# Nine small loads for the left-over rows of W_down in layer two, and fewer unread products in two norms

## The chip, the cores and the metric

The kernel runs on one core of one Trainium2 chip. The core has five engines that run side by side: PE (matrix products; loading its weights is listed apart as PEld), DVE (vector work), ACT (scalar functions and copies), POOL (here only set-up), and SP, which issues the transfers. Transfers run on the core's 16 DMA engines. The metric is the device time of one execution in microseconds; the time before is 730.42, the median of three runs (730.34 to 730.63).

## The reference

Two equal layers are computed, each of them an attention over a cached window and a gated MLP, for a batch of B = 4 with one token each. D = 640, 32 heads of 128, a window of 1024 keys, F = 1728.

```python
x = x + _A_ref(_layernorm(x), A_k_cache, A_v_cache, A_wq, A_wo)
x = x + _B_ref(_layernorm(x), B_W_gate, B_W_up, B_W_down)
x = x + _A_ref(_layernorm(x), A_k_cache, A_v_cache, A_wq, A_wo)
x = x + _B_ref(_layernorm(x), B_W_gate, B_W_up, B_W_down)
# _A_ref: q = x @ wq; softmax(q k^T / sqrt(128)) v over the last 1024 keys; @ wo
# _B_ref: gate = x @ W_gate; h = gate * (gate > 0) * (x @ W_up); h @ W_down
```

All of it is in float32. The weights and the caches are the same in both layers, and there is far more of them than the memory on the core can hold, so most of them are read twice.

## The kernel before

On the host, everything that is read is laid out in rows of 128 partitions: `heads` (q, k, v and o of the first heads), `kept` (those of the last heads), `mlp` (the MLP's weights) and `limbs` (the last 128 keys' values of head 17, cut into pieces of few partitions). A large tile, `store` (128 partitions by 50,624 columns of float32), takes them in turn.

**The loads.** `plan` is a list of loads, each with a layer, a row, a range of columns `lo` to `hi` and a place `to` in `store`. It is written out by hand and worked off in that order. `load()` issues every load at the list's head whose place is free; `live` keeps which columns are still to be read, and `free()` and `done()` call `load()` after each product that frees some. So the program fixes on SP one order of loads, each with the semaphores that it waits for: those of PE or ACT for its place, and one of the eight semaphores DMAHW0 to DMAHW7, which the loads take in turn. A load waits until the earlier load on its own semaphore has landed. SP works its list off in order, so a load that waits holds those behind it.

The `limbs` loads take five rows, or two, at a stride of four partitions. They fill the last 2048 columns of `store` (from 48,576), which `free(STORE - PART, STORE)` gives back after head 17.

**The MLP.** W_down has 1728 rows: three blocks of 512, one of 128, and 64 left-over rows. In `mlp` the left-over rows lie at `TAIL` as 128 partitions by 320 columns: the halves of the 64 rows stand above each other. In layer two the MLP comes by nine loads, with the borders in `cuts`. `forward()` works off `gate(3)`, then `gate(0)`, `gate(1)`, `gate(2)`, each a set of products with W_gate and W_up into `pp`, followed by ACT and DVE (`gated`) and by a transposition of h (`hidden`), and then `down(3)`, `down(0)`, `down(1)`, `down(2)` into y. `gate(3)` and `down(3)` are those of the last 192 columns of F: a block of 128 and the 64 left over. For these, `hidden(3)` turns h by PE into `ph` and copies it to `probs`, and `down(3)` does four products with the left-over rows, each on 64 partitions. At the end y is copied to `probs` and stored.

**The unread products.** `busy(n)` and `fill(n)` put products on PE whose results nobody reads; they do so only while `waits[0]` is true. `normalized()` sets it to true at its start, puts two by `busy` behind the sum of y and one by `fill` behind the mean. It is called four times: in `attention` and in `forward` of both layers.

Of the kernel before, what the change touches and what calls it, by code (L numbers as in the profile page):

```python
# [14 lines left out]
P = 128  # L15
KC = D // P
QUARTER = D // 4
# [44 lines left out]
STORE = 50624  # L62
# [7 lines left out]
FIRST, MOST = 32384, 16192  # L70
LAP = 3 * MOST
SPLIT, PART = 17, 2048
LIMBS = [(half + i, 5, 0, 1536) for i in range(4) for half in (0, 32)] + [(i, 2, 1536, PART) for i in range(4)]
RUNS = [(half, 20, 512 * s, 40 * s + 20 * (half > 0)) for s in range(3) for half in (0, 32)] + [(0, 8, 1536, 120)]

# [37 lines left out]
def decode_kernel(ctx: ExitStack, tc: tile.TileContext, x, source, out):  # L113
# [99 lines left out]
    to = stretch(1, hi, last, 0)  # L213
    for lo, hi in (last, near(last + 12800)), (near(last + 12800), heads_end):
        to = put(1, "heads", to if to + hi - lo <= STORE else 0, lo, hi)
    cuts = [0, 7040, 12160, GU0 + 3 * GU, WD1 + WD, MLP - 4 * D, MLP - 2 * D, MLP - D, MLP - QUARTER, MLP]
    for lo, hi in zip(cuts, cuts[1:]):
        to = put(1, "mlp", to if to + hi - lo <= STORE else 0, lo, hi)

    plan.reverse()  # L220

# [3 lines left out]
    def load():  # L225

        if not held:
            nc.sync.dma_start(out=first_q, in_=source["heads"][:, :HELD])
        while plan:
            layer, row, lo, hi, to = plan[-1]  # L230
            if any(live[to:STORE if row == "limbs" else to + hi - lo]):
                break
            plan.pop()
            if row == "limbs":
                live[to:STORE] = [lo == len(LIMBS) - 1] * PART
                p, n, a, b = LIMBS[lo]
                nc.sync.dma_start(out=store[p:p + 4 * n - 3:4, to + a:to + b], in_=source[row][p:p + 4 * n - 3:4, a:b])  # L237
                continue
            live[to:to + hi - lo] = [True] * (hi - lo)
            held.setdefault((layer, row), []).append((lo, hi - lo, to))  # L240
            nc.sync.dma_start(out=store[:, to:to + hi - lo], in_=source[row][:, lo:hi])
# [128 lines left out]
            nc.tensor.matmul(m[32 * g:32 * g + 32], sel_q, a, start=True, stop=True, tile_position=(0, 32 * g))  # L370
        return m

    def normalized():

        ysb, xc, sq = probs[:, :QUARTER], gates[:, :QUARTER], gates[:, QUARTER:2 * QUARTER]
        waits[0] = True
        nc.vector.tensor_reduce(su, y, axis=AX.X, op=ALU.add)
        nc.scalar.copy(ysb, y)
        busy(2)
        mu = mean(su)  # L380
        nc.vector.tensor_tensor(xc, ysb, mu.to_broadcast([P, QUARTER]), op=ALU.subtract)
        nc.scalar.activation(sq, xc, AF.Square, accum_out=ss)
        fill(1)
        nc.vector.transpose(xT, xc)
        return ss
# [140 lines left out]

    def attention(layer):
        gs = order[layer]
        rstd = deviation(normalized())
        table(AF.Exp)  # L530
        query(layer, gs[0], True)
        query_out(gs[0], rstd)
        query(layer, gs[1])
        query_turned(gs[0])
        go_on()
        query_out(gs[1], rstd)
        scores(layer, gs[0])
        query(layer, gs[2])
        softmax(gs[0])
        query_turned(gs[1])  # L540
        query_out(gs[2], rstd)
        for before, g, after, then in zip([None] + gs, gs, gs[1:] + [None], gs[2:] + [None] * 2):
            totals(g)
            turned()
            if layer == 0 and after is None:
                nc.scalar.copy(probs[:, QUARTER:QUARTER + 768], store[:, AHEAD[0]:AHEAD[1]])
                nc.scalar.copy(ps.rearrange("p j n -> p (j n)"), store[:, BACK[0]:BACK[0] + 1024])
                nc.scalar.copy(yy[:, QUARTER:3 * QUARTER], store[:, BACK[1] - 320:BACK[1]])
                free(*AHEAD)
            if before is not None:  # L550
                values_turned(before)
            if then is not None and before is not None:
                query(layer, then)
                query_out(then, rstd)
            if after is not None:
                scores(layer, after)
                softmax(after)
            else:
                table(AF.Sqrt)
            if then is not None:  # L560
                query_turned(then)

            if before is not None and not (layer == 0 and after is None):
                project(layer, before)
            values(layer, g, after is None)
        values_turned(gs[-1])
        if layer == 0:
            for i in range(2):
                nc.scalar.copy(banks[i][:, P:], away[:, 512 + 384 * i:896 + 384 * i])
            free(*AWAY)  # L570
            project(layer, gs[-2])
        fill(1)
        project(layer, gs[-1], True)

    def forward(layer):
        ss = normalized()
        gus, hTs = {}, {}

        def gate(j):
            n, groups = (P, 4) if j < 3 else (64, 3)  # L580
            at = GU0 + j * GU if j < 3 else 0
            gus[j] = pp[:, j % 2, :2 * P]
            for c in range(KC):
                for g in range(groups):
                    lo = at + (c * groups + g) * 2 * n
                    product(gus[j][32 * g:32 * g + 32], xT[:, 32 * c:32 * c + 32], layer, "mlp", lo, 2 * n,
                            start=c == 0, stop=c == KC - 1, tile_position=(0, 32 * g))
                    done(layer, "mlp", lo, 2 * n)

        def gated(j):  # L590
            n, p = (P, P) if j < 3 else (64, 96)
            gu = gus.pop(j)
            at = P * (j + 1) % 512
            a, b = gates[:p, at:at + n], probs[:, :P] if j < 3 else gates[:p, 3 * P:3 * P + n]
            nc.scalar.activation(a, gu[:p, :n], AF.Relu, scale=rstd[:p])
            nc.vector.scalar_tensor_tensor(b, gu[:p, n:2 * n], rstd[:p], a, op0=ALU.mult, op1=ALU.mult)
            return b

        def hidden(j, h):
            if j < 3:  # L600
                hTs[j] = gates[:, P * j:P * j + P].rearrange("p (f x) -> p f x", f=4)[:, :, :B]
                nc.vector.transpose(gates[:, P * j:P * j + P], h)
                return
            hTs[j] = probs[:, P:P + 2 * B].rearrange("p (f x) -> p f x", f=2)
            ph = bank(P).rearrange("p (f x) -> p f x", f=4)
            for g, lo, f in (0, 0, 0), (1, 64, 0), (2, 0, 1), (2, 64, 1):
                nc.tensor.matmul(ph[lo:lo + 64, f, :B], h, ident[:96, 32 * g:32 * g + B],
                                 start=True, stop=True, tile_position=(0, lo))
            nc.vector.tensor_copy(hTs[j], ph[:, :2, :B])

        def down(j, last=False):
            for f in range(4 if j < 3 else 1):
                lo = WD1 + j * WD + f * D if j < 3 else WD0
                for g in range(4):
                    product(y[32 * g:32 * g + B], hTs[j][:, f], layer, "mlp", lo + g * QUARTER, QUARTER,
                            start=False, stop=last and f == 3, tile_position=(0, 32 * g))
                done(layer, "mlp", lo, D)
                if j == 3:
                    fill(1)
                elif not (last and f > 1):  # L620
                    busy(1)
                if j == 0 and f == 1:
                    fill(2)
            if j == 3:
                for g in range(4):
                    r = slice(64 * (g // 2), 64 * (g // 2) + 64)
                    product(y[32 * g:32 * g + B], hTs[j][r, 1], layer, "mlp", TAIL + g % 2 * QUARTER, QUARTER,
                            start=False, stop=False, rows=r, tile_position=(r.start, 32 * g))
                done(layer, "mlp", TAIL, 2 * QUARTER)

        gate(3)
        waits[0] = layer == 0
        rstd = deviation(ss)
        go_on()
        fill(1)
        h = gated(3)
        for j, j1 in (3, 0), (0, 1), (1, 2):
            gate(j1)
            hidden(j, h)
            fill(1)  # L640
            h = gated(j1)
        down(3)
        down(0)
        hidden(2, h)
        if layer == 0:
            nc.scalar.copy(away[:, :512].rearrange("p (j n) -> p j n", j=2), pp[:, :, 256:])
            for i in range(2):
                nc.scalar.copy(away[:, 512 + 384 * i:896 + 384 * i], banks[i][:, P:])
            live[AWAY[0]:AWAY[1]] = [True] * 1280
        down(1)  # L650
        down(2, last=True)

# [61 lines left out]
```

## Time and profile before

| | us |
|---|---|
| median of three runs | 730.42 |
| the profiled execution | 730.35 |
| its span, from the first to the last instruction | 728.5 |
| attention's last load (128x12672) issued | 660.03 |
| first MLP load of layer two issued | 666.03 |
| last products begin | 724.81 |
| store issued | 725.87 |

In what follows, a row of the timeline has a start, a length, the engine, the line, the operation and its tiles, a count, and in brackets how long the engine stood idle before it and what ended that. "SPq" is SP's list of transfers. A piece of the chain has a start, a length and what the end of the program was waiting for. A row of the waits has the total, the number of times and the longest. A row for a stretch has its borders, its length, PE's busy time with a count, the granted clock of PE as a share of full speed, the mean busy share of the 16 DMA engines (packets are counted where they start, so it can pass 1) and GB/s. Products in float32 have two records each.

### The profile page before, as it was taken

Reading aid. Unit: us, or ns where it says so; the run is one execution under the profiler, and the core shown is the slowest. Engines: PE = TensorE matmul, PEld = TensorE weight load, DVE = VectorE, ACT = ScalarE, POOL = GpSimd, SP = SyncE. Lnnn points to the kernel's source line nnn. Section 1 sums busy time; section 2 is a strip of 40 time slices with the busy share of each in tenths; the row PEclk is TensorE's granted clock in tenths of the full one; section 3 lists DMA queues with packets and bytes.
Section 4 is the critical chain, followed back from the end, with each engine's and each line's share of the span. In section 5 each row is a group of like instructions: output and inputs, shape, how many; then the busy total and the mean of one; then the engine's idle time right before and its main releaser. Section 6 shows DMA issues by size and latency. Waiting matters only on the chain.

```text
span 728.5 us, 8337 instructions
## 1 busy us (share of the span) xinstructions
PE 442.4 (61%) x3816; PEld 142.2 (20%) x3816; DVE 70.0 (10%) x215; ACT 54.2 (7%) x101; POOL 1.8 (0%) x11
## 2 busy tenths in 40 slices
PE   3545564644655475519878896465655556557576
PEld 1111111111111121103333241021111112102123
DVE  2010010000010000002111211001000010001011
ACT  2000000000000000001312210000000000000100
POOL 0000000000000000000000000000000000000000
PEclk9978787977778786759999999677777787859889
DMA  9999999999999999999999999999999999999997
GB/s 406 447 394 447 439 444 444 401 441 437 439 432 421 418 456 421 440 423 429 417 413 413 435 429 448 443 430 436 419 440 436 437 436 415 448 435 430 420 423 301
DMA packets 13482, 311.10 MB, mean 427 GB/s; under 512 B 1572, under 2 KB 1956, under 8 KB 7176
## 3 DMA queue, kind: packets, MB, share of 16 engines
q1 hardware_dynamic: 13440, 310.56, 99.2%
q8 instruction: 30, 0.49, 0.2%
q14 instruction: 4, 0.03, 0.0%
q10 hardware_dynamic: 8, 0.01, 0.0%
HBM read 310.49 MB, written 0.08 MB: 426 GB/s over the span
## 4 chain that ended last, share of the span: by engine, by line
DMA 77%; PE 20%; SPq 1%; issue 1%; DVE 0%; ACT 0%; DVEq 0%
DMA store<-in_heads 61%; PE ps L272 9%; DMA store<-in_kept 8%; DMA store<-in_mlp 8%; PE po L272 6%; PE m L272 2%; PE y L272 1%; PE pp L272 1%; PE pp L457 1%; PE m L428 1%; SPq L237 1%; PE po L486 0%; PE m L513 0%; PE m L504 0%; PE y L400 0%
## 5 line engine op out<-in xcount | busy, mean ns | idle before, releaser
L272 PE MATMUL po<-store,pT 128*16 128x512 f32 (+1 forms) x1024 | 155.8, 712 | 125.5 <-DMA store<-in_heads 118.8
L272 PE MATMUL ps<-store,qT 128*4 128x512 f32 (+3 forms) x996 | 147.5, 676 | 102.4 <-DMA store<-in_heads 81.1
L272 PEld LDWEIGHTS po<-store,pT 128*16 128x16 f32 x1024 | 32.1, 109 | 232.4 <-DMA store<-in_heads 122.4
L272 PEld LDWEIGHTS ps<-store,qT 128*4 128x4 f32 x996 | 29.5, 92 | 202.6 <-DMA store<-in_heads 92.0
L453 ACT ACTIVATE probs<-ps,nm 128x1024 f32<-128x1024 f32 x17 | 18.9, 1113 | 332.9 <-DVE nm L449 332.9
L272 PE MATMUL m<-store,xT 128*32 128x512 f32 (+4 forms) x150 | 29.5, 598 | 23.2 <-DMA store<-in_heads 23.2
L449 DVE TENSOR_REDUCE nm<-ps 128x1 f32<-128x1024 f32 x17 | 20.8, 1225 | 230.1 <-PE ps L272 230.1
L272 PE MATMUL y<-store,oT 128*4 128x160 f32 x512 | 22.0, 305 | 11.0 <-DMA store<-in_heads 9.8
L500 ACT COPY gates<-po 128x512 f32<-128x512 f32 x16 | 9.4, 586 | 259.7 <-PE po L272 259.7
L272 PE MATMUL pp<-store,xT 128*32 128x256 f32 (+3 forms) x322 | 20.1, 350 | 8.7 <-DMA store<-in_mlp 4.2
L466 DVE COPY pT<-pp 128x32 f32<-128x32 f32 x64 | 10.3, 185 | 135.9 <-PE po L272 117.3
L457 PE MATMUL pp<-sel_sb,probs 128*128 128x128 f32 x144 | 20.1, 286 | 0.0
L457 PEld LDWEIGHTS pp<-sel_sb,probs 128*128 128x128 f32 x144 | 17.8, 150 | 0.0
L506 DVE RECIPROCAL r<-m 128x16 f32<-128x16 f32 x18 | 4.6, 257 | 132.0 <-PE m L504 132.0
L272 PEld LDWEIGHTS y<-store,oT 128*4 128x4 f32 x512 | 12.3, 87 | 18.8 <-DMA store<-in_heads 10.1
L421 DVE TENSOR_SCALAR gates<-m,rstd 128x512 f32<-128x512 f32 (+2 forms) x18 | 12.4, 689 | 29.2 <-PE m L272 29.2
L272 PEld LDWEIGHTS pp<-store,xT 128*32 128x32 f32 x322 | 10.4, 109 | 17.0 <-DMA store<-in_mlp 7.6
L272 PEld LDWEIGHTS m<-store,xT 128*32 128x32 f32 x150 | 6.3, 116 | 35.7 <-DMA store<-in_heads 25.8
L428 PE MATMUL m<-sel_sb,gates 128*128 128x128 f32 x64 | 12.7, 324 | 0.0
L513 PE MATMUL m<-sel_sb,gates 128*128 128x128 f32 x72 | 11.7, 284 | 0.8 <-DVE gates L493 0.8
L428 PEld LDWEIGHTS m<-sel_sb,gates 128*128 128x128 f32 x64 | 7.9, 160 | 19.6 <-issue 19.1
L272 PE MATMUL y<-store,gates 128*4 128x160 f32 x192 | 9.8, 299 | 2.2 <-DMA store<-in_mlp 2.1
(82 smaller groups left out, 131.5 us busy)
## 6 DMA issues: line engine op xcount, KB each, us to landing
store<-in_heads SPq DMA_DIRECT2D x15, 7936.0 KB
store<-in_heads SPq DMA_DIRECT2D x3, 8096.0 KB
store<-in_heads SPq DMA_DIRECT2D x3, 7872.0 KB
store<-in_heads SPq DMA_DIRECT2D x2, 8032.0 KB
store<-in_heads SPq DMA_DIRECT2D x1, 8000.0 KB
store<-in_heads SPq DMA_DIRECT2D x1, 7424.0 KB
store<-in_heads SPq DMA_DIRECT2D x1, 7360.0 KB
store<-in_heads SPq DMA_DIRECT2D x1, 7168.0 KB
```

The costliest lines, as they stand in the source:

```text
L237: nc.sync.dma_start(out=store[p:p + 4 * n - 3:4, to + a:to + b], in_=source[row][p:p + 4 * n - 3:4, a:b])
L272: nc.tensor.matmul(out[:, a:z], by, t[rows, p:p + z - a], start=start and not a, stop=stop and z == n, **how)
L421: nc.vector.tensor_scalar(gates[:, :len(HEADS[g]) * P], qp.pop(g), rstd, SCALE, op0=ALU.mult, op1=ALU.mult)
L428: nc.tensor.transpose(qt[:, i], gates[:, i * P:(i + 1) * P], ident)
L449: nc.vector.tensor_reduce(nm[g], to.rearrange("p j n -> p (j n)"), axis=AX.X, op=ALU.max, negate=True)
L453: nc.scalar.activation(probs, sc.pop(g).rearrange("p j n -> p (j n)"), AF.Exp, bias=nm.pop(g), accum_out=sums[g])
L457: nc.tensor.transpose(pp[:, c // 4, c % 4 * P:c % 4 * P + P], probs[:, c * P:(c + 1) * P], ident)
L466: nc.vector.tensor_copy(to, pp.rearrange("p j (c x) -> p (j c) x", c=4)[:, :, i:P:32])
L500: nc.scalar.copy(gates, po)
L506: nc.vector.reciprocal(r[g], so.rearrange("p (b i) -> p i b", b=B)[:, :SIDE])
L513: nc.tensor.transpose(ot[:, 127 * b:127 * b + P], gates[:, b * P:(b + 1) * P], ident)
```

## The change

In layer two, the 64 left-over rows no longer come as 128x320 inside an MLP load. They have a source of their own, `ends`, of 64 partitions by 1280 columns. Rows 0 to 19 and 20 to 39 lie side by side on partitions 0 to 19; rows 40 to 59 lie on partitions 32 to 51, and rows 60 to 63 beside them on partitions 32 to 35. So they lie on 40 partitions, and nine loads bring them: four of 5x1280, four of 5x640 (five rows at a stride of four) and one of 4x640. Their place is the last 1280 columns of `store`, inside the place of the limbs. POOL first zeroes partitions 0 to 31 there, since partitions 20 to 31 are read as well. In `plan` they stand right ahead of the MLP loads of layer two, whose borders move: the 320 columns at `TAIL` are left out.

`hidden(3)` of layer two turns h in six products in place of four, and `down(3)` does the left-over rows in eight products, four on partitions 0 to 51 and four on partitions 0 to 35. Layer one is as before. `normalized` gets a parameter: the three unread products are left out in the first norm (attention of layer one) and in the last (MLP of layer two).

```diff
+ENDS = [(p, 5, 4, 0, 2 * D) for p in range(4)] + [(p, 5, 4, 0, D) for p in range(32, 36)] + [(32, 4, 1, D, 2 * D)]
...
-    cuts = [0, 7040, 12160, GU0 + 3 * GU, WD1 + WD, MLP - 4 * D, MLP - 2 * D, MLP - D, MLP - QUARTER, MLP]
+    cuts = [0, 7040, 12160, TAIL, WD1, WD1 + WD, MLP - 4 * D, MLP - 2 * D, MLP - D, MLP - QUARTER, MLP]
+    plan.append((1, "ends", 0, 2 * D, STORE - 2 * D))
     for lo, hi in zip(cuts, cuts[1:]):
-        to = put(1, "mlp", to if to + hi - lo <= STORE else 0, lo, hi)
+        if lo != TAIL:
+            to = put(1, "mlp", to if to + hi - lo <= STORE else 0, lo, hi)
...
+            if row == "ends":
+                live[to:to + hi] = [True] * hi
+                nc.gpsimd.memset(store[:32, to:to + hi], 0.0)
+                for p, n, by, a, b in ENDS:
+                    rows = slice(p, p + by * (n - 1) + 1, by)
+                    nc.sync.dma_start(out=store[rows, to + a:to + b], in_=source[row][rows, a:b])
+                continue
...
-    def normalized():
+    def normalized(warm):
...
-        waits[0] = True
+        waits[0] = warm
...
-        rstd = deviation(normalized())
+        rstd = deviation(normalized(layer > 0))
...
-        ss = normalized()
+        ss = normalized(layer == 0)
...
-            for g, lo, f in (0, 0, 0), (1, 64, 0), (2, 0, 1), (2, 64, 1):
-                nc.tensor.matmul(ph[lo:lo + 64, f, :B], h, ident[:96, 32 * g:32 * g + B],
+            turns = [(0, 0, 0, 0, 64), (1, 64, 0, 0, 64)]
+            turns += [(2, 0, 1, 0, 32), (2, 0, 2, 20, 32), (2, 32, 1, 40, 20), (2, 32, 2, 60, 4)] if layer else [
+                (2, 0, 1, 0, 64), (2, 64, 1, 0, 64)]
+            for g, lo, f, first, n in turns:
+                nc.tensor.matmul(ph[lo:lo + n, f, :B], h[:, first:first + n], ident[:96, 32 * g:32 * g + B],
...
-            if j == 3:
+            if j == 3 and layer:
+                for s, rows in enumerate((52, 36)):
+                    for g in range(4):
+                        at = STORE - 2 * D + s * D + g * QUARTER
+                        nc.tensor.matmul(y[32 * g:32 * g + B], hTs[j][:rows, 1 + s], store[:rows, at:at + QUARTER],
+                                         start=False, stop=False, tile_position=(0, 32 * g))
+                free(STORE - 2 * D, STORE)
+            elif j == 3:
```

The order of the loads on SP, from attention's last two loads to the store of the result, before the change (each with the semaphores that it waits for; PE, DVE and Activation are those engines' own):

```order
L241 DMA store<-in_heads 128x12800 [waits DMAHW1_49,PE_49]
L241 DMA store<-in_heads 128x12672 [waits DMAHW7_49,DMAHW2_49,PE_49]
L241 DMA store<-in_mlp 128x7040 [waits DMAHW3_49,DMAHW0_49,PE_49]
L241 DMA store<-in_mlp 128x5120 [waits DMAHW4_49,PE_49]
L241 DMA store<-in_mlp 128x5120 [waits DMAHW5_49,PE_49]
L241 DMA store<-in_mlp 128x3520 [waits DMAHW6_49,DMAHW1_49,PE_49]
L241 DMA store<-in_mlp 128x2560 [waits PE_49]
L241 DMA store<-in_mlp 128x1280 [waits PE_49]
L241 DMA store<-in_mlp 128x640 [waits PE_49]
L241 DMA store<-in_mlp 128x480 [waits DMAHW2_49,PE_49]
L241 DMA store<-in_mlp 128x160 [waits DMAHW3_49]
L657 DMA out_x<-probs 128x160 [waits DMAHW4_49,DVE_49,Activation_49]
```

The same place on SP with the change, from attention's last load to the third MLP load:

```order
L251 DMA store<-in_heads 128x12672 [waits DMAHW7_49,DMAHW2_49,PE_49]
L242 DMA store<-in_ends 5x1280 [waits DMAHW3_49,Pool_49]
L242 DMA store<-in_ends 5x1280 [waits DMAHW4_49]
L242 DMA store<-in_ends 5x1280 [waits DMAHW5_49]
L242 DMA store<-in_ends 5x1280 [waits DMAHW6_49]
L242 DMA store<-in_ends 5x640
L242 DMA store<-in_ends 5x640 [waits DMAHW0_49]
L242 DMA store<-in_ends 5x640 [waits DMAHW1_49]
L242 DMA store<-in_ends 5x640 [waits DMAHW2_49]
L242 DMA store<-in_ends 4x640 [waits DMAHW3_49]
L251 DMA store<-in_mlp 128x7040 [waits DMAHW4_49,PE_49]
L251 DMA store<-in_mlp 128x5120 [waits DMAHW5_49,PE_49]
```

The load that took DMAHW2 last is 128x12672 itself, one place ahead of the small loads. Before, the next load on DMAHW2 was the eighth MLP load (480 columns); now it is the eighth small load, and all MLP loads stand behind it. The ninth small load waits for the first one (DMAHW3), and the 7040 columns wait for the second (DMAHW4).

On PE, the last norm and the MLP's beginning before the change (`po<-sel_sb` are the unread products, `m` the means, `pp<-store` the products of the gates):

```order
L272 MATMUL y<-store,oT 4x160 x12
L354 MATMUL po<-sel_sb 128x128 x2
L370 MATMUL m_123<-ones,sel_sb 32x1 x4
L361 MATMUL po<-sel_sb 128x128
L272 MATMUL pp<-store,xT 32x128 x15
L370 MATMUL m_124<-ones,sel_sb 32x1 x4
L400 MATMUL y<-probs,sel_sb 128x160
L272 MATMUL pp<-store,xT 32x256 x20
L607 MATMUL m_123<-sel_sb,gates 64x4 x4
L272 MATMUL pp<-store,xT 32x256 x40
L272 MATMUL y<-store,probs 4x160 x8
```

The same place on PE with the change:

```order
L282 MATMUL y<-store,oT 4x160 x12
L380 MATMUL m_123<-ones,sel_sb 32x1 x4
L282 MATMUL pp<-store,xT 32x128 x15
L380 MATMUL m_124<-ones,sel_sb 32x1 x4
L410 MATMUL y<-probs,sel_sb 128x160
L282 MATMUL pp<-store,xT 32x256 x20
L620 MATMUL m_123<-sel_sb,gates 64x4 x2
L620 MATMUL m_123<-sel_sb,gates 32x4 x2
L620 MATMUL m_123<-sel_sb,gates 20x4
L620 MATMUL m_123<-sel_sb,gates 4x4
L282 MATMUL pp<-store,xT 32x256 x40
L641 MATMUL y<-store,probs 4x160 x8
```

The unread products are gone from between the sums and the means, the turned products of h are six in place of four, and the products with the left-over rows are eight in place of four (in the rows before, they are the second half of the eight with `probs`).

More of the change, by code (lines that the diff above doesn't have):

```diff
@@ L603, in hidden @@
                 return
-            hTs[j] = probs[:, P:P + 2 * B].rearrange("p (f x) -> p f x", f=2)
+            hTs[j] = probs[:, P:P + 3 * B].rearrange("p (f x) -> p f x", f=3)
             ph = bank(P).rearrange("p (f x) -> p f x", f=4)
-            for g, lo, f in (0, 0, 0), (1, 64, 0), (2, 0, 1), (2, 64, 1):
-                nc.tensor.matmul(ph[lo:lo + 64, f, :B], h, ident[:96, 32 * g:32 * g + B],
+            turns = [(0, 0, 0, 0, 64), (1, 64, 0, 0, 64)]
[3 more added lines that the diff above has]
+                nc.tensor.matmul(ph[lo:lo + n, f, :B], h[:, first:first + n], ident[:96, 32 * g:32 * g + B],
                                  start=True, stop=True, tile_position=(0, lo))
-            nc.vector.tensor_copy(hTs[j], ph[:, :2, :B])
+            nc.vector.tensor_copy(hTs[j][:, :2 + layer], ph[:, :2 + layer, :B])
         def down(j, last=False):
@@ L682 @@
         limbs[p:p + m, at:at + 512] = split[key:key + m]
+    last = arr(B_W_down)[3 * 512 + P:]
+    ends = np.zeros((64, 2 * D), np.float32)
+    for row, at, first, m in (0, 0, 0, 20), (0, D, 20, 20), (32, 0, 40, 20), (32, D, 60, 4):
+        ends[row:row + m, at:at + D] = last[first:first + m]
     laid = {row: np.concatenate([parts[what][i] for what, i in row_of], axis=1) for row, row_of in PARTS.items()}
@@ L701 @@
         "limbs": limbs,
+        "ends": ends,
     }
@@ L706 @@
             for n, a in arrays.items()}
-    source = {n: args[n] for n in ("heads", "kept", "mlp", "limbs")}
+    source = {n: args[n] for n in ("heads", "kept", "mlp", "limbs", "ends")}
     out = nc.dram_tensor("out_x", (P, QUARTER), F32, kind="ExternalOutput").ap()
```

## The prediction

> **What bounds the kernel now.** I read the page from the top: the busy shares and the DMA row, then the chain, then the queue's own waits, then the last 90 us as a timeline.
>
> ```profile
> span 728.5 us, 8337 instructions
> PE 442.4 (61%) x3816; PEld 142.2 (20%) x3816; DVE 70.0 (10%) x215; ACT 54.2 (7%) x101; POOL 1.8 (0%) x11
> DMA  9999999999999999999999999999999999999997
> DMA packets 13482, 311.10 MB, mean 427 GB/s; under 512 B 1572, under 2 KB 1956, under 8 KB 7176
> DMA 77%; PE 20%; SPq 1%; issue 1%; DVE 0%; ACT 0%; DVEq 0%
> ```
>
> No engine is busy for more than 61%, but the transfers fill every slice to 90% or more until the last: 311 MB at 427 GB/s are 728 us, the span itself. So time is won by moving fewer bytes or keeping the queue full, and it is lost wherever the queue runs dry. Work on PE, DVE and ACT is hidden as long as it ends before its data.
>
> The end of the chain and a few single rows of the timeline show the stage that the change touches:
>
> ```profile
> 660.03 34.15 DMA store<-in_heads
> 694.25 30.52 DMA store<-in_mlp
> 724.81 0.65 PE y L272 x8
> 694.25 0.33 SPq L241 DMA_DIRECT2D store<-in_mlp  x1
> 702.51 0.33 SPq L241 DMA_DIRECT2D store<-in_mlp  x1
> 666.03 36.81 SPq L241 DMA_DIRECT2D store<-in_mlp  x9
> SPq L241 <- DMA store<-in_heads: 9.5, 1, 9.5
> ```
>
> The last load of attention, 128x12672, is issued at 660.03 and has landed at 694.18. The nine MLP loads are issued from 666.03 on, that is 28 us before the queue reaches them, and so their bytes follow without a gap: the last lands at 694.25 + 30.52 = 724.77, and 25,920 columns of 512 bytes (13.27 MB) in those 30.6 us are 434 GB/s. Behind it stand four products, the copy and the store.
>
> The row at 694.25 matters most. It is the eighth MLP load (480 columns). In the program's order it waits for DMAHW2, and it stands eight loads behind 128x12672, which is the load that used that semaphore last. The loads take eight semaphores in turn, so **a load is held until the load eight places ahead has landed**, and 9.5 us of such waiting are in the last row above (the queue's waits between 693 and 695). For this load it is harmless, since seven loads are queued already. The row at 702.51 is the ninth load, which waits in the same way for the first MLP load (7040 columns); that one has thus landed at about 702.47.
>
> **The change part by part.**
>
> *The nine small loads.* They stand between 128x12672 and the first MLP load. The first seven wait for semaphores of loads that land before 694 (the latest is 128x12800, for which PE waited until 679.00, in the last row of the next fence), so they are issued early. The eighth (5x640) takes DMAHW2 and is held until 128x12672 has landed: 694.25. The ninth and all MLP loads stand behind it on SP. At that moment nothing but 160 KB of small loads is left in the queue, so **all sixteen DMA engines run dry**. What an issue of such a load costs is shown by the limbs (five rows each, then two), and what a start from an empty queue costs by the first load of the program (pieces of the chain, rows of the timeline, an issue with its size, and two stretches with PE's busy time, granted clock, DMA share and GB/s):
>
> ```profile
> 605.91 0.71 SPq L237
> 606.66 0.66 SPq L237
> 609.27 0.56 SPq L237
> 609.94 34.91 DMA store<-in_heads
> 0.73 0.38 SPq L228 DMA_DIRECT2D first_q<-in_heads  x1
> 8.29 4.06 PE L272 MATMUL m<-first_q,xT 128*32 128x512 f32 x24 [2.32 <-DMA first_q<-in_heads]
> first_q<-in_heads SPq DMA_DIRECT2D x1, 2144.0 KB
> 0.00:1.70 1.70, 0.00 (x0) 1.00 0.01 5
> 1.70:2.40 0.70, 0.00 (x0) 1.00 1.64 371
> 679.00 2.76 PE L272 MATMUL po<-store,pT 128*16 128x512 f32 x12 [7.04 <-DMA store<-in_heads]
> ```
>
> - Issue: 0.66 and a gap of 0.04 for the eighth. The ninth has four rows, between 0.56 and 0.66, say 0.62, and 0.10 to the next issue (609.27 + 0.56 to 609.94). The 7040 columns are issued at 694.25 + 0.70 + 0.72 = 695.67.
> - Start: first_q is issued at 0.73 and PE goes on at 8.29, so it landed at 8.25: 7.52 us for 2144 KB. The 7040 columns are 3520 KB, 1.41 MB more, at 434 GB/s 3.25 us. They land at 695.67 + 7.52 + 3.25 = 706.44, against 702.47: **3.97 us later**.
> - Rest: before, 18,880 columns took from 702.47 to 724.77, 22.30 us. Now it is 18,560, as the 320 left-over columns are out: 21.92 us. The last load lands at 728.36: **+3.59**.
>
> The start is the only price that the trace shows but once, so I bound it. From below: transfers begin at 1.70 (the two stretches), 0.97 after the issue. Full speed from there on and a landing with no delay would put the 7040 columns at 695.67 + 0.97 + 8.31 = 704.95 and the end at +2.1. From above: both issues at 0.71, and the same start, +3.7. I take +3.6, the measured row.
>
> The rows of the timeline for the other parts are these:
>
> ```profile
> 650.25 6.36 PE L272 MATMUL po<-store,pT 128*16 128x512 f32 x32
> 0.73 0.23 POOL L305 MEMSET sel_sb<- 128x160 f32 x1 [0.29 <-POOLq L704]
> 705.90 0.24 PE L370 MATMUL m<-ones,sel_sb 128*32 128x1 f32 x8
> 707.03 1.18 PE L272 MATMUL pp<-store,xT 128*32 128x128 f32 x27 [0.47 <-DVE xT L384]
> 712.88 2.37 PE L272 MATMUL pp<-store,xT 128*32 128x256 f32 x40 [0.54 <-DVE probs L596]
> 716.12 2.37 PE L272 MATMUL pp<-store,xT 128*32 128x256 f32 x40 [0.87 <-DVE probs L596]
> 718.87 0.84 PE L272 MATMUL y<-store,probs 128*4 128x160 f32 x16 [0.38 <-DMA store<-in_mlp]
> 719.63 1.27 PE L272 MATMUL y<-store,gates 128*4 128x160 f32 x32
> 721.99 1.27 PE L272 MATMUL y<-store,gates 128*4 128x160 f32 x32 [1.09 <-DMA store<-in_mlp]
> 723.51 1.15 PE L272 MATMUL y<-store,gates 128*4 128x160 f32 x24 [0.25 <-DMA store<-in_mlp]
> ```
>
> *More products in down(3).* Four row-split products of 160 columns become eight, and four turned products of h become six. The row at 719.63 has sixteen products in 1.27 us (two records each), so four more are 0.3 us, and two short ones no more than that, beside a queue that PE waits for anyway. The copy grows from 8 to 12 columns. Nothing, unless PE is late in this stage. The zeroing on POOL (32x1280) waits for the limbs' last reader, at 650.25, and even ten times the start's 0.23 us for 160 columns would be over before 660.03.
>
> *The unread products of two norms.* In the first norm they end long before PE waits for first_q at 8.29. In the last, PE waits for DVE at 705.90 and at 707.03 with them or without. I cost both at nothing; what covers them is the transfer that PE waits for afterwards. The gain is nothing too, because no instruction stands waiting behind them.
>
> *PE behind the late data.* With 434 GB/s from 706.44, the next 5120 columns land at 712.48, in time for the products at 712.88; the 5760 land at 719.28, where the products of 716.12 need them. PE then stands idle from 715.25 to 719.28, 4.0 us. The trace has a like case:
>
> ```profile
> 694.23 8.26 PE L272 MATMUL po<-store,pT 128*16 128x512 f32 x42 [4.52 <-DMA store<-in_heads]
> 694.00:696.00 2.00, 1.77 (x12) 0.50 0.98 422
> 700.00:702.00 2.00, 2.00 (x18) 0.95 0.86 371
> ```
>
> After 4.52 us of idleness the granted clock is 0.50 for 6 us of work. Six us at half speed lose 3 us. From 719.28 to 728.36 there are 9.08 us for 2.37 + 0.84 + 1.27 + 1.27 + 1.15 = 6.9 us of products, 2.2 of slack. So the loss is between nothing and 0.8 us. I take 0.2, as the clock may fall late in the wait and come back earlier. [...]
>
> **The sum.** Profiled execution: 730.35, of it 728.5 span and 1.85 around it. 730.35 + 3.6 + 0.2 = 734.1. The median of the runs shown, 730.42, is 0.07 above the profiled one, so nothing is corrected.
>
> **The rivals.**
>
> 1. *The queue does not run dry (not slower).* Then only the bytes count. The left-over columns ride on few partitions and leave the other DMA engines free: 320 of 25,920 columns of 30.6 us, 0.38 us less, 729.97. For it: the engines do not finish together, so there is slack that small loads can fill.
>
> ```profile
> 720.00:722.00 2.00, 0.91 (x30) 1.00 0.88 361
> 722.00:723.00 1.00, 1.00 (x32) 1.00 0.80 317
> 723.00:724.00 1.00, 0.75 (x24) 1.00 0.54 206
> 724.00:725.00 1.00, 0.85 (x22) 1.00 0.23 75
> ```
>
> The share falls over 4 us instead of at once. And the limbs at 605.91 are such loads without a visible stop; but there a 128x15872 load stood in the queue behind the landed one. It is decided by when the 7040 columns are issued: before about 691.7 (the start's 7.52 less 5.06 for its bytes is 2.46 us ahead of 694.18) they cost nothing. That needs the eighth small load not to wait for 128x12672, and the program's rows say that it does. [...] Chance 0.04.
>
> 2. *The stop is shorter.* The queue takes new loads while it drains, and the start costs 0.97 us, not 2.46: +2.1, or less with one issue hidden, 731.7 to 732.5. For it, only the stretch rows above. Chance 0.10.
>
> 3. *PE becomes the bound.* If the granted clock falls at 719 and stays half to the end, 6.9 us of products take 13.8, and the end comes at 719.28 + 13.8 + 1.3 for the last four products, against 725.46: +9. The row at 700 speaks against it, since PE got its clock back after 6 us of work. Half of that, with a slow packet or two, gives 735.5 to 738. Chance 0.08.
>
> The forecast, a dry queue with the measured start, holds the rest, 0.78.
>
> **How the numbers follow.** A measurement of this kernel can tell about 0.2% from no change, which is 1.5 us, so "same" is 728.96 to 731.88. Rival 1 lies in it, and so does the lower part of rival 2: same 0.07. Faster needs a gain that no row offers: 0.02. Slower 0.91. The range goes from 732.2, the lower bound of the start, to 735.8, the forecast with the whole loss of the clock and a little more.
>
> **What would show it.** Between 694 and 698 the DMA share of the stretches should fall to nearly nothing, where it was 0.92 to 1.04. SP should issue the eighth small load at about 694.3 and the 7040 columns at about 695.7, and the last products should begin at 728.4 to 729. PE should wait some 4 us for the 5760 columns. The time up to 694 should not change. The forecast is wrong if the MLP loads are issued before 694, or if the share stays up between 694 and 698.

## The result and the profile after

The changed kernel takes 734.94 us (median of six runs, 734.72 to 735.16) against 730.34 for the kernel before on the same chip: 1.0062 times as long, with an interval from 1.0051 to 1.0073, or 4.6 us more. The profiled execution took 735.15, of which 733.3 is the span; 1.85 lie around it, as before.

The page after, its busy shares, the DMA rows and the GB/s by slices:

```profile
span 733.3 us, 8366 instructions
PE 450.9 (61%) x3820; PEld 146.1 (20%) x3820; DVE 70.1 (10%) x215; ACT 54.2 (7%) x101; POOL 2.9 (0%) x12
DMA  9999999999999999999999999999999999999897
GB/s 403 444 433 402 444 441 435 441 436 412 442 434 435 415 456 416 440 424 426 418 412 413 440 425 452 426 437 440 434 434 436 420 431 436 440 445 414 335 406 302
DMA packets 13572, 311.11 MB, mean 424 GB/s; under 512 B 1617, under 2 KB 2001, under 8 KB 7265
```

The bytes are the same 311 MB. One slice of the DMA row has fallen from 9 to 8, the third from the right, and its GB/s are 335 where its neighbours have 414 and 406. A slice is 18 us long, so a stop of a few microseconds is all that one sees of it here.

The end of the chain of the changed kernel, then single rows of its timeline on SP's list, then on PE:

```profile
658.87 35.25 DMA store<-in_heads
...
698.92 30.65 DMA store<-in_mlp
729.57 0.04 issue
729.62 0.63 PE y L282 x8
```

```profile
659.29 36.02 SPq L242 DMA_DIRECT2D store<-in_ends  x9
694.14 1.17 SPq L242 DMA_DIRECT2D store<-in_ends  x2
694.84 0.47 SPq L242 DMA_DIRECT2D store<-in_ends  x1
695.43 0.36 SPq L251 DMA_DIRECT2D store<-in_mlp  x1
706.41 0.33 SPq L251 DMA_DIRECT2D store<-in_mlp  x1
```

```profile
706.53 2.14 PE L282 MATMUL pp<-store,xT 128*32 128x128 f32 x27 [1.66 <-DMA store<-in_mlp]
720.63 3.49 PE L282 MATMUL pp<-store,xT 128*32 128x256 f32 x40 [2.50 <-DMA store<-in_mlp]
```

Attention's last load lands at 694.12, within 0.1 us of the time before. The eighth small load goes out at 694.14, the ninth at 694.84, and the first MLP load (7040 columns) at 695.43, where it went out at 666.03 before. It lands at 706.4 in place of 702.5, and the last load at 729.57 in place of 724.77. The queue between, in stretches (PE's busy time with a count, its granted clock, the DMA share, GB/s):

```profile
690.00:692.00 2.00, 0.35 (x3) 1.00 0.77 332
692.00:694.00 2.00, 0.00 (x0) 1.00 0.16 62
694.00:696.00 2.00, 1.83 (x12) 0.60 0.06 18
696.00:698.00 2.00, 2.00 (x12) 0.54 0.86 239
```

Before, the share was 0.92 to 1.04 in all four. Now it is 0.16 and 0.06 for 4 us: little is in transfer but the small loads and the last packets of attention. What SP waits for meanwhile, with a small load at the head of its list, is attention's last load (from the waits between 685 and 700):

```profile
SPq L242 <- DMA store<-in_heads: 14.2, 1, 14.2
```

### The profile page after: what moved, and what is told of

It reads as the page before. It is cut to its first block, busy times and chain, and to the rows that moved or that the text cites. A ratio compares the mean times of both kernels' runs of the same rounds, so it can differ in the third digit from the quotient of the medians.

```text
span 733.3 us, 8366 instructions
## 1 busy us (share of the span) xinstructions
PE 450.9 (61%) x3820; PEld 146.1 (20%) x3820; DVE 70.1 (10%) x215; ACT 54.2 (7%) x101; POOL 2.9 (0%) x12
## 4 chain that ended last, share of the span: by engine, by line
DMA 77%; PE 21%; issue 1%; DVE 0%; SPq 0%; ACT 0%; DVEq 0%
DMA store<-in_heads 60%; DMA store<-in_kept 9%; PE ps L282 8%; DMA store<-in_mlp 8%; PE po L282 7%; PE m L282 2%; PE y L282 1%; PE pp L282 1%; PE pp L467 1%; PE m L438 1%; PE po L496 0%; PE m L523 0%; PE m L514 0%; SPq L251 0%; PE y L410 0%
## 5 line engine op out<-in xcount | busy, mean ns | idle before, releaser
L282 PE MATMUL po<-store,pT 128*16 128x512 f32 (+1 forms) x1024 | 159.3, 729 | 123.2 <-DMA store<-in_heads 117.3
L282 PE MATMUL pp<-store,xT 128*32 128x256 f32 (+3 forms) x322 | 24.5, 411 | 11.0 <-DMA store<-in_mlp 8.4
L282 PEld LDWEIGHTS pp<-store,xT 128*32 128x32 f32 x322 | 12.5, 125 | 20.7 <-DMA store<-in_mlp 7.7
```

The lines of the kernel that those rows point to most:

```text
L282: nc.tensor.matmul(out[:, a:z], by, t[rows, p:p + z - a], start=start and not a, stop=stop and z == n, **how)
```

## The experiments

Two theories stood to be told apart. Mine was that the loss is the stop of the queue, made by a wait for a semaphore ("dry queue" in the expectations). The rivals were that the small loads cost by themselves (few DMA engines carry them, twice the products, their issues) and that PE's clock suffers without the unread products. The times are medians, and each ratio is against the kernel before on the same chip (730.32 to 730.41).

### The unread products alone

The kernel before with `normalized(warm)` as in the change, and nothing else:

```diff
-        waits[0] = True
+        waits[0] = warm
...
-        rstd = deviation(normalized())
+        rstd = deviation(normalized(layer > 0))
...
-        ss = normalized()
+        ss = normalized(layer == 0)
```

> The kernel before with only the three unread products left out in the first and in the last norm. Dry queue (my theory: the eighth small load waits for attention's last load, and all MLP loads wait behind it): nothing, 730.2 to 730.5. Rival, the products held PE's clock up and their absence is what costs: most of the 4.6 us, 733 to 735, with a lower granted clock between 704 and 725.

Measured: 730.40 us, ratio 1.0001 (0.9992 to 1.0009). The other side of the same question is the changed kernel with the products put back (`normalized(True)` in both places):

> The changed kernel with the unread products back in the first and the last norm. Dry queue: 734.7 to 735.2, as the changed kernel, and again one or two DMA engines that end about 1.2 us behind the others (a DMA share of 0.10 to 0.15 in the last microsecond of the loads). Rival, part of the 4.6 us comes from PE's clock, which the unread products would hold up: 733.5 to 734.3.

Measured: 734.96 us, ratio 1.0063 (1.0049 to 1.0076), the changed kernel's time. So the products cost and bring nothing here. They do hold up PE's clock, though. Stretches around the last norm, first of the kernel before, then two of the kernel before without the products, then of the changed kernel and of the changed kernel with the products put back, and last a row of the timeline on PE of the kernel before without the products:

```profile
704.00:710.00 6.00, 4.18 (x84) 1.00 1.01 433
```

```profile
704.00:710.00 6.00, 4.20 (x72) 0.72 1.00 429
710.00:718.00 8.00, 6.58 (x124) 1.00 0.99 421
```

```profile
704.00:710.00 6.00, 3.66 (x53) 0.55 0.96 414
```

```profile
704.00:710.00 6.00, 3.90 (x78) 1.00 0.96 413
```

```profile
706.03 2.14 PE L272 MATMUL pp<-store,xT 128*32 128x128 f32 x27 [0.89 <-DVE xT L384]
```

Without them the mean granted clock of the stretch is 0.72 in place of 1.00 (0.55 in the changed kernel), and the first products of the gates take 2.14 us in place of 1.18. In the kernel without the products alone the DMA share is 1.00 and 0.99 all the while, and the time is the same to 0.1 us: what PE loses there, it does not lose at the last load.

### The order of the loads alone

The changed kernel, with four small loads, then the 7040 columns, then the other five:

```diff
-    plan.append((1, "ends", 0, 2 * D, STORE - 2 * D))
+    plan.append((1, "ends", 0, 4, STORE - 2 * D))
     for lo, hi in zip(cuts, cuts[1:]):
...
+        if lo == 0:
+            plan.append((1, "ends", 4, 9, STORE - 2 * D))
...
```

> The changed kernel with the order of the loads alone altered: four small loads, the 7040 MLP columns, then the other five small loads. The 7040 columns then take a semaphore that is free at 666, and 3.5 MB stand in the queue while the eighth small load waits for attention's last load. Dry queue: the stop is gone, 729.5 to 730.5, no DMA share under 0.8 between 690 and 700. Rival, the small loads themselves cost (they burden the few DMA engines that carry them, 33 KB more on each, 1.2 us, or the doubled products): 731.5 or more, even without a stop.

Measured: 730.74 us, ratio 1.0007 (0.9998 to 1.0015). Its rows on SP, and its stretches:

```profile
666.16 0.34 SPq L254 DMA_DIRECT2D store<-in_mlp  x1
666.54 29.37 SPq L245 DMA_DIRECT2D store<-in_ends  x5
696.03 0.82 SPq L254 DMA_DIRECT2D store<-in_mlp  x2
```

```profile
692.00:694.00 2.00, 0.00 (x0) 0.74 0.91 389
694.00:696.00 2.00, 1.93 (x12) 0.50 1.01 436
696.00:698.00 2.00, 2.00 (x12) 0.50 0.95 408
```

The same nine loads, the same bytes and products, and 4.2 us of the 4.6 are gone, because the 7040 columns go out at 666.16 and are in transfer while SP waits. The time is 0.2 over the range that I had written for it, and the 0.38 us that the prediction's first rival gave the small loads as a saving did not come.

### Loads that nobody reads

The kernel before, with small loads (5x32) whose data nobody reads put ahead of its MLP loads; its computation is unchanged. They have next to no bytes (0.6 KB each) and no products, so only their issues and their places in the list count.

```diff
+    plan.append((1, "spare", 0, 7, STORE - 2 * D))
...
+            if row == "spare":
+                for i in range(hi):
+                    nc.sync.dma_start(out=store[0:17:4, to + 64 * i:to + 64 * i + 32], in_=source["limbs"][0:17:4, 0:32])
+                continue
```

Seven of them:

> The kernel before with seven added loads of 5x32 that nobody reads ahead of the MLP loads; the computation is that of before. The 7040 columns then take the semaphore of attention's last load and wait for it. Dry queue: they are issued at 694.2 and land at 694.2 + 7.5 + 3.25 = 705.0 in place of 702.5, so the end is 2.5 later, 732.9, and up to 1.3 more if the DMA engines, once they start level, are held up by single slow packets that a spread of starts hid before. Rival, it is the bytes or the products of the left-over rows: 730.3 to 730.8, as 3 KB and no product are added.

Measured: 734.59 us, ratio 1.0059 (1.0044 to 1.0075). That is 0.4 over the top of what I had written, 734.2. Six:

> As the run before, with six added loads in place of seven. The 7040 columns then take the semaphore of the 128x12800 load, which lands at 679, and are issued at 679 behind a full queue; the next MLP load waits until 694.2 while they are in transfer. Dry queue: 730.2 to 730.6, as before. Rival, each small load costs its issue or a disturbance of its own: six sevenths of what the run before costs, 732 to 733.5.

Measured: 730.72 us, ratio 1.0008 (0.9999 to 1.0017), 0.1 over the range. Fifteen:

> The kernel before with fifteen added unread loads of 5x32 ahead of the MLP loads; the computation is that of before. The eighth waits for attention's last load, and it and seven more are issued ahead of the 7040 columns, 0.70 each. Dry queue: those columns are issued at 694.1 + 8 x 0.70 = 699.7 in place of 694.07 with seven added loads, so the time is 5.6 over that run, 740.2. Rival, the loss is one stop of the queue of a given length, whatever stands behind it: 734.6, as with seven.

Measured: 739.87 us, ratio 1.0129 (1.0114 to 1.0145), 0.3 under the forecast.

The rows on SP, with seven, with six and with fifteen added loads:

```profile
694.07 0.34 SPq L246 DMA_DIRECT2D store<-in_mlp  x1
704.93 0.33 SPq L246 DMA_DIRECT2D store<-in_mlp  x1
```

```profile
680.88 0.34 SPq L246 DMA_DIRECT2D store<-in_mlp  x1
695.83 1.28 SPq L246 DMA_DIRECT2D store<-in_mlp  x3
```

```profile
694.72 5.57 SPq L237 DMA_DIRECT2D store<-in_limbs  x8
700.39 4.33 SPq L246 DMA_DIRECT2D store<-in_mlp  x8
```

One load more, 0.6 KB that nobody reads, and the time goes up by 3.9 us: with six the 7040 columns take the semaphore of the 128x12800 load and go out at 680.88, with seven they take that of attention's last load and go out at 694.07. (The profiled execution with six is one of 732.29 us; PE had the 128x12800 load at 680.86 in it, and at 679.00 before.) Eight more add 5.28 us, where eight issues of 0.70 (5.57 us in the row) stand ahead of the columns. So the price is not that of a small load; it is the time that the queue stands empty, and behind the wait every issue counts nearly in full. The sixth to seventh step also shows how easily it is met: nothing in the code of the loads tells which semaphore one will take.

### Fewer loads for the same rows

If the count is at fault, fewer loads for the same places should do. The changed kernel with three in place of nine:

```diff
-ENDS = [(p, 5, 4, 0, 2 * D) for p in range(4)] + [(p, 5, 4, 0, D) for p in range(32, 36)] + [(32, 4, 1, D, 2 * D)]
+ENDS = [(0, 20, 1, 0, 2 * D), (32, 20, 1, 0, D), (32, 4, 1, D, 2 * D)]
```

> The changed kernel with the same 64 rows in the same places by three loads (20x1280, 20x640, 4x640) in place of nine. The 7040 columns then take a semaphore that is free early. Dry queue: no stop, 730.0 to 730.6. Rival, what costs is that the left-over rows come ahead of the MLP, on few partitions, with twice the products: 734 to 735, as nine loads gave.

Measured: 731.82 us, ratio 1.0021 (1.0012 to 1.0030). Neither theory had this. There is no stop, as the rows on SP and the share show:

```profile
660.21 1.02 SPq L242 DMA_DIRECT2D store<-in_ends  x3
666.67 0.35 SPq L251 DMA_DIRECT2D store<-in_mlp  x1
```

```profile
690.00:692.00 2.00, 0.00 (x0) 1.00 1.10 401
692.00:694.00 2.00, 0.00 (x0) 0.66 0.85 247
694.00:696.00 2.00, 0.68 (x4) 0.50 0.92 284
696.00:698.00 2.00, 2.00 (x16) 0.50 1.02 436
```

The 7040 columns go out at 666.67, and the DMA engines are busy for 85% and more. But they move only 247 and 284 GB/s for 4 us: they are busy and slow. Against 434 that is (187 + 150) x 2 / 434 = 1.55 us, the 1.5 that is missing. Besides their number, two things differ from the nine loads: the rows lie on partitions beside each other, where those have a stride of four, and a load of twenty rows is spread over more engines than one of five. The page's packets under 512 B show the spread if, as I read the trace, each engine ends its part of a load with one packet of 4 bytes (of the 1572 in the kernel before, 1568 are in the queue of these loads: sixteen for each of 92 transfers of 128 partitions, and for each limb as many as it has rows, five or two; the nine small loads add 44): 24 are added by these three loads (1572 before, 1596 here), that is ten, ten and four. Two kernels with the same bytes and four loads each tell the partitions from the rest; both put the 64 rows on partitions 0 to 31, in two halves side by side, and so need no zeroing:

```diff
-ENDS = [(p, 5, 4, 0, 2 * D) for p in range(4)] + [(p, 5, 4, 0, D) for p in range(32, 36)] + [(32, 4, 1, D, 2 * D)]
+ENDS = [(p, 8, 4, 0, 2 * D) for p in range(4)]
...
-                nc.gpsimd.memset(store[:32, to:to + hi], 0.0)
...
-                for s, rows in enumerate((52, 36)):
+                for s, rows in enumerate((32, 32)):
...
```

> The changed kernel with the 64 rows side by side in two halves on partitions 0 to 31, by four loads of 8x1280, each at a stride of four partitions (p, p+4, ... p+28); no zeroing, six of the eight doubled products' rows fewer. Dry queue: the 7040 columns take a semaphore that is free at 666, no stop, 730.0 to 730.8. [...] Rival, anything but a load of 128 partitions slows the others: 731.5 to 732.5, as with three loads.

Measured: 730.68 us, ratio 1.0008 (0.9999 to 1.0017). And with the rows of each load beside each other:

```diff
-ENDS = [(p, 8, 4, 0, 2 * D) for p in range(4)]
+ENDS = [(8 * p, 8, 1, 0, 2 * D) for p in range(4)]
```

> As the run before, the same four loads of 8x1280, the same bytes, but each on eight partitions that lie beside each other (0 to 7, 8 to 15 and so on). Partitions: eight engines write to eight neighbouring partitions at once, and the packets of all engines near them are slow again, GB/s under 350 in some stretch between 690 and 698 with a DMA share over 0.8: 731.3 to 733. Rival, in the three loads it was the number of rows or of engines: 730.0 to 730.8, as the run before.

Measured: 732.23 us, ratio 1.0025 (1.0015 to 1.0035). The stretches, first at a stride of four, then beside each other:

```profile
692.00:694.00 2.00, 0.00 (x0) 0.77 0.93 393
694.00:696.00 2.00, 1.73 (x12) 0.50 1.04 451
```

```profile
692.00:694.00 2.00, 0.00 (x0) 0.84 0.86 257
694.00:696.00 2.00, 0.94 (x8) 0.50 0.96 333
```

The order of the loads is the same, and so are the bytes and the number of engines (32 packets under 512 B are added in both, 1572 to 1604, eight for each load). Where the rows lie makes 1.55 us: ten of eleven executions at a stride of four took 731.18 at most (one took 733.28), and all of the other kernel took 731.75 or more. In the trace it is the large load beside the small ones that slows: its packets of 28,160 bytes take 1044 ns each between 688 and 700 at a stride of four, and up to 1642 ns with the rows beside each other. The rows are neighbours in their source too, so these two runs do not show at which end of the transfer the slowness arises, nor what makes it.

No kernel tried here beats the one before. The four that keep the queue full and the rows apart (the products alone, the altered order, six unread loads, the stride of four) lie 0.0 to 0.4 us over it, and the intervals of their ratios all take in 1.

## Why the prediction was right, point by point

- **The hold at 694.25.** Right: the eighth small load went out at 694.14, just after attention's last load had landed. Six and seven unread loads show that it is the semaphore's turn that decides, and the altered order of the same nine loads leaves only 0.3 us for all else in them. The hole lies somewhat earlier than I had written (694 to 698): the engines come to the end of attention's load one after another (from 689.8 to 693.7, by the trace's packets), so the share is down to 0.77 between 690 and 692 already, and it is back at 0.86 between 696 and 698.
- **The issues, 1.42 us.** 1.29 (694.14 to 695.43). The ninth load, with four rows, took 0.47, less than any bound I had set for it. Fifteen unread loads confirm 0.70 for one of five rows.
- **The start from an empty queue.** From its issue the 7040 columns took 10.9 us to land (695.43 to 706.4), and I had 10.77 by the program's first load; with seven unread loads it was 10.8 (694.07 to 704.9). Rival 2, a start of 0.97 us, falls. So the columns came 3.9 us later, as forecast. The trace's packets show where the price lies. The first of the 7040 columns starts at 696.40, which is 0.97 after the issue, as at the program's start; but the first sixteen take 1.14 to 1.96 us each, where such a packet takes 1.04 in the kernel before. In these first microseconds the columns move at 239 GB/s (the row 696 to 698), and rival 2 had them at full speed.
- **The rest, 21.92 us.** This term was too small: 23.2 (706.4 to 729.57), 1.3 more, and with seven unread loads 23.6 in place of 22.3, again 1.3 more. I had let the rest run at the rate of before. So the last products began at 729.62, later than the 728.4 to 729 that I had named. The end of the loads shows where it went, in the changed kernel and then in the one with seven unread loads:

```profile
727.00:728.00 1.00, 1.00 (x32) 1.00 0.84 307
728.00:729.00 1.00, 0.73 (x24) 1.00 0.15 58
729.00:730.00 1.00, 0.82 (x20) 1.00 0.12 30
```

```profile
726.00:727.00 1.00, 0.95 (x29) 1.00 0.90 332
727.00:728.00 1.00, 0.77 (x20) 1.00 0.15 56
728.00:729.00 1.00, 0.81 (x16) 1.00 0.10 24
```

A share of 0.10 to 0.15 is two of sixteen engines. The trace's packets say the same; here is when each engine's part of the last load was through, worked out from them:

```
kernel before      720.8 721.0 721.6 722.9 723.0 723.2 723.2 723.4 723.8 723.8 724.2 724.3 724.4 724.6 724.6 724.7
changed kernel     727.5 727.5 727.7 727.7 727.8 727.8 727.8 727.8 727.9 727.9 728.0 728.0 728.0 728.3 729.4 729.4
seven unread loads 726.7 726.7 726.7 726.7 726.8 726.8 726.8 726.9 726.9 726.9 727.0 727.1 727.2 727.2 728.1 728.3
```

Before, the engines end over 4 us, and they already lie 3.8 us apart where they come to the 7040 columns (689.9 to 693.7). In the changed kernel they start almost level after the stop (the first sixteen packets between 696.40 and 697.34), and fourteen end within 0.8 us of each other, but two are held up in the last 30 us and end 1.1 behind the last of these; the kernels with fifteen unread loads and with the products put back end in the same way. Single packets with half a microsecond more than their like are in these records, before (849 ns in place of 385 at 719.39, 1229 in place of 761 at 710.73) and after (862 in place of 385 at 725.33, 1229 in place of 761 at 711.27). That a spread of lags had hidden such delays, as the queue never made the engines wait for each other, is my reading of these three rows; no run tested it by itself.

- **PE behind the late data, 0.2.** It came to nothing: the last products began 0.05 after the last load had landed. Rival 3 falls. The wait and the loss of clock behind it did come, but the slack took them in. The changed kernel with the unread products put back shows them best:

```profile
718.00:725.00 7.00, 4.36 (x44) 0.54 0.96 403
```

```profile
720.64 4.49 PE L282 MATMUL pp<-store,xT 128*32 128x256 f32 x40 [4.74 <-DMA store<-in_mlp]
```

PE waits 4.74 us for the 5760 columns, where I had 4.0, and the products behind it take 4.49 us in place of 2.37. In the changed kernel itself that wait is only 2.50 us and the products take 3.49, because an earlier fall of the clock had made PE late already:

```profile
710.19 4.49 PE L282 MATMUL pp<-store,xT 128*32 128x256 f32 x40 [0.42 <-DVE gates L606]
```

The trace has that fall at 704.65, ahead of the wait for the 7040 columns and after 3.41 us (701.24 to 704.65; no change of the clock in this trace comes sooner after the one before) in which PE was busy for 1.90, so idleness alone did not make it. The kernel before without the unread products, where no data are late, falls likewise (705.68) but is back at full clock at 709.09, in place of 714.89 here; with the products put back there is no fall before 718. So the missing products make this fall, and the late data may have prolonged it. The prediction did not have it. The granted clock of 0.54 to 0.60 from 694 to 698 is no sign of the change, as it was 0.50 there before.

- **The unread products and the doubled ones at nothing.** Right for both in time: 0.0 for the first, measured alone, and at most 0.3 for the second with everything else of the small loads, in the kernel with the altered order.
- **Rival 1**, the queue kept full, is what the altered order makes of the change. It then came out at +0.3 instead of -0.38. The time that the bytes save on most engines was not the time that ends the loads. From the packets of the changed kernel, the five engines that carry the small loads reach them between 691.9 and 693.5, in the midst of the others (689.9 to 693.7 before), and each takes 33 KB in place of 10. That they had no lead to spend is thus likely, but it was not tried alone.

The sum of the profiled executions: +4.8 at the last load (724.77 to 729.57) and +4.8 in the time (730.35 to 735.15); forecast were +3.6 and 0.2 for PE. That the time lies within the range, 732.2 to 735.8, is in part luck: its upper part was there for the loss of the clock, which cost nothing, and it took in the 1.3 us that the rest ran longer, which I had not foreseen.

## What to carry to other kernels

Where transfers are the bound, a load costs by what stands queued behind it when it has to wait, and not by its size: count which semaphore each load will take, and keep a large transfer in the queue whenever a load that waits for the last one is at the list's head. Here one unread load of 0.6 KB more cost 3.9 us, and the same nine loads around a large one cost 0.3. Small loads on a few partitions should have their rows at a stride (four here) and not beside each other, which cost 1.55 us. Moving bytes onto few engines saved nothing here; that it pays only if these have a lead is likely, but not shown.

## What the runs showed of the hardware that was not expected

- Small loads of neighbouring rows slow the large transfers beside them: 247 to 333 GB/s for 4 us at a busy share of 0.85 to 0.96, against 393 to 451 with a stride of four and the same bytes.
- An issue of five rows at a stride of four takes twice that of 128 partitions: 0.66 us against 0.33 to 0.36, and one of four rows 0.47. Three loads of 20, 20 and 4 neighbouring rows were out in 1.02 us altogether.
- After a nearly common start, two of sixteen DMA engines end 0.8 to 1.2 us behind the last of the others some 30 us later, in each of the four profiles with a stop.
